# Batch 1's w1 and wo sums as transposed blocks on TensorE, with its kept heads at places 24 to 28 of the second pass

## The chip, the cores and the metric

The kernel runs on one core of one Trainium2 chip. The time is the device time of one execution in microseconds, from the first to the last instruction of that core; where several runs are compared, their median is meant.

## The reference

The reference is one decode step of a transformer block and all its gradients. There are B = 2 batch rows, D = 640, H = 32 heads of 128, caches of Sk = 4096 positions for each batch row and head, and Dff = 1728. Everything is bfloat16.

```python
def _fwd_reference(A_x, A_k_cache, A_v_cache, A_wq, A_wo, B_x, B_w1, B_w2):
    ...
    x = A_x
    h = x + _A_ref(_layernorm(x, axis=-1), A_k_cache, A_v_cache, A_wq, A_wo)
    h2 = h + _B_ref(_layernorm(h, axis=-1), B_w1, B_w2)
    return h2
...
_out, _vjp = jax.vjp(_f, A_x, A_k_cache, A_v_cache, A_wq, A_wo, B_w1, B_w2)
_grads = _vjp(grad_out)
```

`_A_ref` is attention of one query per head over its cache, and `_B_ref` is `relu(h @ w1) @ w2`. The outputs are the block's result and the gradients of x, of both caches, of wq, wo, w1 and w2. The two caches are read (128 MB in bfloat16), and gradients of the same size are written. For each head the gradient of V is an outer product of the softmax row with the incoming gradient `go`, and the gradient of K is an outer product of the score gradient with the query. The score gradient needs V times `go`, so V is read a second time once `go` is known.

`go` of a head is the matrix `wo` of that head times the gradient `gh1` of the middle row h. `gh1` in turn needs w1 times the gradient of the hidden layer. These two products, w1 (640 x 1728) times a vector and wo (4096 x 640) times a vector, are what the change moves.

## The kernel before

**Two passes over the heads.** The program is written out by a loop over a plan. Pass 1 (`p1_iter`) takes the 64 pairs of batch row and head in order: it transposes K tiles on TensorE (`transpose_group`, L415), forms scores and exponentials and sums V. Pass 2 (`p2_iter`) takes them in the order of a list `turns`: place j of this list is one turn. Pass 2 starts when batch 0 is known, while pass 1 still runs over batch 1; from place 13 on it runs alone.

**A turn of pass 2.** TensorE forms two row broadcasts (L844), then four groups of four float32 transposes of the V tile `Wt` (`pair_transpose`, L436), which ScalarE copies to SBUF (L441), and then the small products with `go` (`pair_matvec`, L449). VectorE makes the two gradient tiles in halves (`outer_half`, L822, named gV and gK), with a small `gsp` (L835) before gK. The GpSimd queue stores the two tiles of 1 MB (L879 for gV, L860 for gK). One V tile of 1 MB is loaded by the Sync queue (L457) for a later turn. For a turn, `bg_until` makes sure that the `go` of its head stands in the program before it.

**Kept heads.** The V tiles of the last 6 heads of batch 0 and the last 5 of batch 1 stay in SBUF from pass 1 (`KEPT`), so their turns in pass 2 need no load. They are the first places of each batch: 0 to 5, and 32 to 36.

**Buffers.** Twelve SBUF tiles of 1 MB have tags: "ld" for loads, "g" for gradients, "f" for finished weight gradients on their way out, "q" for wq and w2 tiles of the last stage. `give` hands a tile back, and `share(...)` sets how many each tag should have; a tile that is given back goes to a tag that lacks one. From place 36 on (`j >= H + KEPT[1] - 1`) the aim is 4 ld, 4 g, 3 f and 2 q. Loads are issued in a fixed order by `pump`, whenever an "ld" tile is free.

**Background work.** Three queues of generators are advanced a little after each step of a turn, each at a rate that is a sort of credit per step:

- the first (`middle_gen`) does the middle of the block for a batch row: the MLP, the w1 sums, `gh1`, and then the `go` groups of heads (`go_group`). For batch 1 it begins with place 13. Both sums are done on VectorE: the vector is spread over all partitions as a row (`bcast_cols`: TensorE products into PSUM, L633, and ScalarE copies, L636), and then `ttr` (L649) multiplies a block of w1 or a head of wo with this row and adds up along it.
- the second (`fin_gen`, rate RATE2) makes the gradients of w2, w1, wo and wq (`outer_rows`): products of two rows in bank tiles with the role "o" (L926), copies to a tile `ot` (L935 on ScalarE, and L933 on VectorE when `late` is set), and stores from the Activation queue.
- the third (`gx_gen`, rate RATE3) makes the gradient of x: once all `go` are done it loads wq tiles (`wqs`, L971), transposes them on TensorE (L993), copies them (L995) and multiplies (L1003).

The last two begin when the w1 sums of batch 1 are done, since their buffers take the place of w1. `mlp_out`, after the `go` groups, loads the w2 tiles and makes the block's result (L709).

**PSUM.** Transposes of both passes alternate between banks 0 and 1 ("tps"). "o" has banks 4, 5 and 6; while `gx_gen` accumulates, it holds bank 6.

Of the kernel before, what the change touches and what calls it, by code (L numbers as in the profile page):

```python
# [7 lines left out]
FP32 = mybir.dt.float32  # L8
# [7 lines left out]
def kernel(  # L16
# [34 lines left out]
    GT = 8  # L51
# [6 lines left out]
    def f_kc(c):  # L58
        return 128 if c < NFF else F_rem
# [332 lines left out]
    NP1 = len(pairs)  # L392
    KEPT = (6, 5)
    turns = [(b, h) for b in range(B) for h in (*range(H - KEPT[b], H), *range(H - KEPT[b]))]
    turn_of = {bh: j for j, bh in enumerate(turns)}
    kept = {(b, h) for b in range(B) for h in range(H - KEPT[b], H)}
    u_bank = [None]
# [256 lines left out]
    def turn():  # L654

        while slot[0] <= 0:
            yield 0.0
        slot[0] -= 1

    def one(src, b):  # L660
        return src[:, :, b]

    def go_group(b, h0, h1, hbc):

        hs = slice(h0, h1)
        n = h1 - h0
        go32 = small.tile([128, GH], FP32, tag="go32", bufs=1, name="go32")
        for k in range(n):
            yield from turn()
            ttr(wo_t[:, h0 + k, :], hbc[:], go32[:, k:k + 1], D)  # L670
            yield 0.9
        nc.vector.tensor_copy(out=goc[:, hs, b], in_=go32[:, 0:n])
# [20 lines left out]
        yield  # L693

    def mlp_out():

        ml32 = small.tile([128, ND, B], FP32, tag="ml32", bufs=1, name="ml32")
        nc.vector.memset(ml32[:], 0.0)
        for k in range(NW2):
            while free["q"] < 1:  # L700
                yield
            t = load_w2(k, "q", "(p c) d -> p c d")
            yield from wait(12)
            c1 = min(NF, (k + 1) * FP)
            m_ps = pst([128, ND, B], FP32, "mid", "mlp_ps")
            for c in range(ND):
                for cf in range(k * FP, c1):
                    kc = f_kc(cf)
                    nc.tensor.matmul(m_ps[:, c, :], lhsT=t[0:kc, cf - k * FP, c * 128:(c + 1) * 128],  # L709
                                     rhs=arow[0:kc, cf, :], start=(cf == k * FP), stop=(cf == c1 - 1))  # L710
            give(t)
            yield
            nc.vector.tensor_tensor(out=ml32[:], in0=m_ps[:], in1=ml32[:], op=ALU.add)
        ml_bf = small.tile([128, ND, B], BF16, tag="ml_bf", bufs=1, name="ml_bf")
        nc.vector.tensor_copy(out=ml_bf[:], in_=ml32[:])
        y_bf = small.tile([128, B, ND], BF16, tag="y_bf", bufs=1, name="y_bf")
        nc.vector.tensor_tensor(out=y_bf[:].rearrange("p b c -> p c b"), in0=h1c[:], in1=ml_bf[:], op=ALU.add)
        yield from wait(3)
        for b in range(B):
            store_row(y_bf[:, b, :], ND, out_0[b].rearrange("s (c p) -> (s c) p", p=128))  # L720
            yield

    def middle_gen(b):
        if o_next[0] < (b + 1) * H // OG:
# [44 lines left out]
        fbc = cols.tile([128, Dff], BF16, tag="fbc", name="fbc")  # L769
        gx2 = small.tile([128, 1, ND], FP32, tag="gx2", bufs=1, name="gx2")  # L770
        gx2p = small.tile([128, ND, 3], FP32, tag="gx2p", bufs=1, name="gx2p")
        FW = Dff // 3
        spread_f = bcast_cols(one(ghfc, b), NF, f_kc, fbc)
        have = 0
        for k in range(3):
            while have < min(Dff, (k + 1) * FW):
                next(spread_f)
                have += 512
                yield
            for c in range(ND):  # L780
                yield from turn()
                ttr(w1_t[:, c, k * FW:(k + 1) * FW], fbc[:, k * FW:(k + 1) * FW], gx2p[:, c, k:k + 1], FW)
                yield 0.85
        nc.vector.reduce_sum(out=gx2[:, 0, :], in_=gx2p[:], axis=AX.X)
        yield ("w1", b)
        yield from ln_bwd(gx2[:], x2c[:, :, b:b + 1], rstd2[:, b:b + 1], gc[:, :, b:b + 1], gh1c[:, :, b:b + 1], 1)
        hbc = cols.tile([128, D], BF16, tag="rowbc", name="hbc")
        yield from bcast_cols(one(gh1c, b), ND, lambda c: 128, hbc)
        yield ("gh1", b)

        first = H - KEPT[b]
        bounds = [(first, first + 2), (first + 2, H)] if b == 0 else [(first, H)]
        bounds += [(h, min(first, h + GH)) for h in range(0, first, GH)]
        for h0, h1 in bounds:
            yield from go_group(b, h0, h1, hbc)
        if b > 0:
            yield from mlp_out()

# [166 lines left out]
    def gx_gen(fin):  # L965
# [11 lines left out]
        for c in range(ND):  # L977
            while c >= len(tiles) or (step[0] < tiles[c][1] + 16 and not forced[0]):
                fetch()
                yield 0.0  # L980
            if acc is None:
                banks["o"].remove(6)
                acc = ps.tile([128, ND, B], FP32, tag="bank6", bufs=1, name="gx_ps")
            t = tiles[c][0]
            todo = list(range(H))
            prev = None
            for t0 in range(0, len(todo) + GT, GT):
                part = todo[t0:t0 + GT]
                nxt = None
                if part:  # L990
                    t_ps = pst([128, GT, 128], BF16, "tps", "t_ps")
                    for x, h in enumerate(part):
                        nc.tensor.transpose(t_ps[:, x, :], t[:, h * 128:(h + 1) * 128], ident_bf[:])  # L993
# [12 lines left out]
                prev = nxt  # L1006
# [50 lines left out]
    M0_ITERS = 7  # L1057
    P2_AT = H + 2 + M0_ITERS
    RATES = (0.2, 0.8, 0.2, 0.8, 0.45)
    RATE2 = 0.65  # L1060
    RATE3 = 0.45
    plan = []
    i = j = 0
    while i <= NP1 + 1 or j <= NP1:
# [60 lines left out]
    for n, (i, j) in enumerate(plan):  # L1125
# [4 lines left out]
            share(ld=KEPT[1] + 3, g=4)  # L1130
        if fin is not None and not bg2 and not bg3:
            share(ld=7, g=6)
        elif fin is not None and j >= H + KEPT[1] - 1:
            share(ld=4, g=4, f=3, q=2)
        if j is not None:
            while g2 is not None:
# [4 lines left out]
        if i is None and ("w1", 1) in done and fin is None:  # L1141
            wts.release()
            fin = tc.alloc_tile_pool(name="fin", bufs=1)
            big2 = tc.alloc_tile_pool(name="big2", bufs=1)
            more_home("f", big2)
            banks.update(sps=[2, 3], o=[4, 5, 6])
            bg2.append(("fin", fin_gen(fin)))
            bg3.append(("gx", gx_gen(fin)))
        late[0] = all(("go", B - 1, h) in done for h in range(H))
# [84 lines left out]
```

## Time and profile before

| what | value |
|---|---|
| time, median of 3 runs | 942.42 us (935.63 to 942.82) |
| span of the profiled run | 939.0 us, mean granted TensorE clock 0.778 |
| busy: PE, PE loads of weights, DVE, ACT, POOL | 82, 68, 70, 59, 15% |
| moved by DMA | 363.02 MB, mean 387 GB/s |
| HBM read, written | 212.16 MB, 149.13 MB |
| chain that ended last | PE 39%, DMA 29%, DVE 15%, ACT 10%, issue 5% |

Busy shares are of the whole span, and pass 1 and pass 2 have different limits, so they don't tell what one stage waits for. The chain's shares name what ended each wait. Two views by stage are of more use: the page's 40 slices of the span, and the table of stretches, which gives each engine's busy time, the granted TensorE clock, and the bytes moved per second between two times. Pass 2 starts at 271 us (the first L844), place 13 at 483 us, place 17 at 519, place 34 at 655 and the last place, 63, at 921 us.

### The profile page before, as it was taken

The page shows a single profiled execution, that of the slowest core. Times are in us where ns is not written, and L with a number is a line of the kernel's source. Part 1 is how long each engine was busy: PE and PEld are TensorE (multiplying, and loading weights), DVE is VectorE, ACT ScalarE, POOL GpSimd, SP SyncE. Part 2 cuts the span into 40 slices and gives each one's busy share as a digit, 9 for nine tenths or more (in the row PEclk, how much of TensorE's full clock was granted, in tenths as well). Part 3 has the DMA queues.
Part 4 walks back from the last instruction along what each step waited for, and adds up shares of the span by engine and source line. Part 5 has one row for each costly group of instructions (what it writes and reads, how often), then busy time and mean ns, then how long its engine had stood idle before and what let it go on. Part 6 is the DMA issues. An engine that isn't in the chain of part 4 may idle for free.

```text
span 939.0 us, 26775 instructions
## 1 busy us (share of the span) xinstructions
PE 766.9 (82%) x11482; PEld 641.4 (68%) x11482; DVE 661.9 (70%) x1237; ACT 551.0 (59%) x1162; POOL 141.0 (15%) x249
## 2 busy tenths in 40 slices
PE   6999898999998888988867838676988877887883
PEld 5878787888787777877757727564766665665652
DVE  4555677766876877786768889787797455465675
ACT  4666565667775776776633626444665564565652
POOL 1222111121001101010012112111121111021111
PEclk9999999999998999998886856556555575575556
DMA  8999999997878999999989999999999999999998
GB/s 348 418 399 410 406 394 410 412 418 266 308 280 341 360 389 423 425 422 414 419 328 369 405 426 395 395 391 376 397 406 398 425 425 423 354 389 377 333 423 364
DMA packets 59478, 363.02 MB, mean 387 GB/s; under 512 B 5696, under 2 KB 15552, under 8 KB 19168
## 3 DMA queue, kind: packets, MB, share of 16 engines
q1 hardware_dynamic: 37920, 212.18, 57.6%
q0 software_dynamic: 18432, 134.23, 34.7%
q10 hardware_dynamic: 3008, 14.91, 4.0%
q8 instruction: 90, 1.47, 0.6%
q14 instruction: 28, 0.23, 0.1%
HBM read 212.16 MB, written 149.13 MB: 385 GB/s over the span
## 4 chain that ended last, share of the span: by engine, by line
PE 39%; DMA 29%; DVE 15%; ACT 10%; issue 5%; POOL 0%; SPq 0%; POOLq 0%; DVEq 0%; ACTq 0%
DMA Kt<-in_A_k_cache_dram 12%; DMA out_dram<-gV 10%; PE t_ps L436 9%; PE m_ps L470 7%; PE t_ps L415 6%; ACT t_sb L420 5%; DMA out_dram<-gK 5%; DVE gV L822 5%; PE s_ps L426 4%; PE o_ps L926 3%; DVE gK L822 3%; DVE pk L477 2%; PE u_ps L495 2%; ACT t_sb L441 2%; DVE junk L649 2%
## 5 line engine op out<-in xcount | busy, mean ns | idle before, releaser
L420 ACT COPY t_sb<-t_ps 128x1024 bf16<-128x1024 bf16 x223 | 216.7, 1012 | 46.6 <-PE t_ps L415 41.8
L441 ACT COPY t_sb<-t_ps 128x512 f32<-128x512 f32 x256 | 149.9, 588 | 159.3 <-PE t_ps L436 156.4
L436 PE MATMUL t_ps<-ident_f,Wt 128*128 128x128 f32 x848 | 195.5, 378 | 3.7 <-ACT t_sb L995 1.4
L470 PE MATMUL m_ps<-pk,Vt 128*128 128x129 bf16 x2048 | 193.3, 224 | 1.0 <-DVE pk L477 0.6
L477 DVE TENSOR_TENSOR pk<-Kt,ep 128x2048 bf16<-128x2048 bf16 x128 | 156.3, 1221 | 34.6 <-ACT ep L520 34.5
L822 DVE TENSOR_TENSOR gK<-rb,gsp 128x2048 bf16<-128x2048 bf16 x128 | 152.2, 1224 | 32.2 <-DMA out_dram<-gK 20.1
L415 PE MATMUL t_ps<-ident_bf,Kt 128*128 128x128 bf16 x2048 | 156.8, 229 | 16.7 <-DMA Kt<-in_A_k_cache_dram 16.6
L822 DVE TENSOR_TENSOR gV<-rb,pp 128x2048 bf16<-128x2048 bf16 x128 | 152.7, 1218 | 23.3 <-DMA out_dram<-gV 20.2
L436 PEld LDWEIGHTS t_ps<-ident_f,Wt 128*128 128x128 f32 x848 | 135.8, 196 | 34.2 <-issue 23.5
L470 PEld LDWEIGHTS <-Vt 128*128 128x128 bf16 x2048 | 130.0, 100 | 29.1 <-issue 29.1
L415 PEld LDWEIGHTS <-Kt 128*128 128x128 bf16 x2048 | 129.3, 102 | 19.1 <-DMA Kt<-in_A_k_cache_dram 18.7
L449 PEld LDWEIGHTS <-t_sb 128*128 128x128 bf16 x2048 | 95.8, 106 | 40.1 <-ACT t_sb L441 18.5
L426 PE MATMUL s_ps<-qc,t_sb 128*128 128x1 bf16 x2048 | 89.2, 164 | 18.1 <-ACT t_sb L420 16.6
L449 PE MATMUL dp_ps<-gom,t_sb 128*128 128x2 bf16 x2048 | 95.2, 167 | 8.9 <-ACT t_sb L441 7.8
L426 PEld LDWEIGHTS <-t_sb 128*128 128x128 bf16 x2048 | 76.0, 97 | 30.6 <-ACT t_sb L420 27.4
L879 POOL DMA_DIRECT2D out_dram<-gV x64 | 34.2, 534 | 288.9 <-DVE gV L822 228.6
L860 POOL DMA_DIRECT2D out_dram<-gK x64 | 34.0, 531 | 279.8 <-DVE gK L822 224.7
L566 POOL COPY P_bf<-ep 128x32 bf16<-128x32 bf16 x40 | 42.6, 1065 | 220.1 <-ACT ep L520 220.1
L935 ACT CAST ot<-o_ps 128x512 bf16<-128x512 f32 (+4 forms) x134 | 60.2, 478 | 23.1 <-DMA out_dram<-ot 11.9
L561 DVE TENSOR_REDUCE rmax<-s_ps 128x1 bf16<-128x32 f32 x64 | 12.3, 193 | 61.4 <-PE s_ps L426 61.3
L649 DVE CUSTOM_DVE_ANT_0 junk<-wo_t,hbc 128x640 bf16<-128x640 bf16 x64 | 52.3, 817 | 0.2
L582 ACT CAST MT<-m_ps 128x128 bf16<-128x128 f32 x64 | 17.1, 267 | 59.1 <-PE m_ps L470 59.1
(194 smaller groups left out, 812.7 us busy)
## 6 DMA issues: line engine op xcount, KB each, us to landing
Kt<-in_A_k_cache_dram SPq DMA_DIRECT2D x64, 1024.0 KB, 14.2
Vt<-in_A_v_cache_dram SPq DMA_DIRECT2D x64, 1024.0 KB, 11.5
out_dram<-gV POOLq DMA_DIRECT2D x64, 1024.0 KB, 10.9
out_dram<-gK POOLq DMA_DIRECT2D x64, 1024.0 KB, 10.3
Wt<-in_A_v_cache_dram SPq DMA_DIRECT2D x53, 1024.0 KB, 10.8
wo_t<-in_A_wo_dram SPq DMA_DIRECT2D x4, 1280.0 KB, 14.1
wqs<-in_A_wq_dram SPq DMA_DIRECT2D x5, 1024.0 KB
wq_t<-in_A_wq_dram SPq DMA_DIRECT2D x5, 960.0 KB, 16.1
```

Of the source, the lines that this page charges most:

```text
L415: nc.tensor.transpose(t_ps[:, j, :], nat[:, g * GT + j, :], ident_bf[:])
L420: nc.scalar.copy(out=t_sb[:], in_=t_ps[:])
L426: nc.tensor.matmul(dst[:, sc:sc + 1], lhsT=t_sb[:, j, :], rhs=vec, start=True, stop=True)
L436: nc.tensor.transpose(t_ps[:, j, :], natf[:, 2 * cc:2 * cc + 2, :].rearrange("p c k -> p (c k)"), ident_f[:])
L441: nc.scalar.copy(out=t_sb[:], in_=t_ps[:])
L449: nc.tensor.matmul(dst[:, sc:sc + 2], lhsT=v[:, j, :, par], rhs=vecs[:, par, :], start=(par == 0), stop=(par == 1))
L470: nc.tensor.matmul(r["m"][:, 0:129], lhsT=r["V"][:, sc, :], rhs=r["pk"][sc // HALF][:, sc % HALF, 0:129], start=(sc == 0), stop=(sc == NSC ...
L477: nc.vector.tensor_tensor(out=p["pk"][k][:, :, 0:128].rearrange("p s (a two) -> p s a two", two=2), in0=p["K"][:, sl, :].rearrange("p s (a ...
L566: (nc.gpsimd if i < P2_AT else nc.vector).tensor_copy(out=P_bf[:, bhp, :], in_=ep[:, :, 0])
L649: nc.vector.tensor_tensor_reduce(out=junk[0:kc, 0:width], in0=in0, in1=in1, scale=1.0, scalar=0.0, op0=ALU.mult, op1=ALU.add, accum_out=acc)
L822: nc.vector.tensor_tensor(out=pairs_view(dst[:, sl, :]), in0=row.rearrange("p (a two) -> p a two", two=2)[:, None, :, :].to_broadcast([128 ...
L935: nc.scalar.copy(out=ot[0:P, k, n0:n0 + nn], in_=o_ps[0:P, 0:nn])
```

## The change

Four things change together.

1. For batch 1, the w1 and wo sums go to TensorE. `turned` transposes blocks of 128 x 128 of the weight (up to eight into one bank), lets ScalarE copy them, and one group later multiplies each with the column that holds the vector, accumulating in bank 6. `gx2_turned` does so for w1 (10 groups), `go_turned` for wo (32 groups, one for each head). Batch 0 keeps the sums on VectorE (`gx2_rows`, `go_group`). The row broadcasts for batch 1 go.
2. The five kept heads of batch 1 come at places 24 to 28 of the second pass, and the batch 0 heads that stood there come at 29 to 36.
3. The buffers are shared out anew from place 28 on in place of 36, so that "f" and "q" get theirs earlier.
4. RATE2 and RATE3, at which the second and third queue advance, are lower, so that this work, which begins earlier, is spread over more turns. "o" has two banks until `gx_gen` gives it bank 6.

In the program's order the w1 sums are then complete at place 19 (before: 22), the first `go` group of batch 1 at place 22 (26), the last at 33 (41); the first wq tile and the first w2 tile are asked for at place 33 (41), and `gx_gen` ends at place 53 (59). `fin_gen` ends at place 61 (60).

```diff
+    KEPT1_AT = 24
+    turns[KEPT1_AT:H + KEPT[1]] = turns[H:H + KEPT[1]] + turns[KEPT1_AT:H]
...
+    def turned(groups, cost):
+
+        prev = None
+        for parts in (*groups, None):
+            if prev is not None:
+                for x, (_, kc, dst, vec, first, last) in enumerate(prev[1]):
+                    nc.tensor.matmul(dst, lhsT=prev[0][0:kc, x, :], rhs=vec, start=first, stop=last)
+            if parts is not None:
+                t_ps = pst([128, GT, 128], BF16, "tps", "t_ps")
+                for x, (src, kc, *_) in enumerate(parts):
+                    nc.tensor.transpose(t_ps[0:kc, x, :], src, ident_bf[:])
+                t_sb = mats.tile([128, GT, 128], BF16, tag="XT", bufs=5, name="t_sb")
+                whole = sum(kc == 128 for _, kc, *_ in parts)
+                nc.scalar.copy(out=t_sb[:, 0:whole, :], in_=t_ps[:, 0:whole, :])
+                for x, (_, kc, *_) in enumerate(parts):
+                    if kc < 128:
+                        nc.scalar.copy(out=t_sb[0:kc, x, :], in_=t_ps[0:kc, x, :])
+                prev = (t_sb, parts)
+            yield cost
+
+    def go_turned(b, h0, h1):
+
+        acc = ps.tile([128, GH], FP32, tag="bank6", bufs=1, name="go_ps")
+        yield from turned([[(wo_t[:, h, c * 128:(c + 1) * 128], 128, acc[:, h - h0:h - h0 + 1],
+                             gh1c[:, c, b:b + 1], c == 0, c == ND - 1) for c in range(ND)]
+                           for h in range(h0, h1)], 1.2)
+        yield from go_done(b, h0, h1, acc)
...
+        if b == B - 1:
+            yield from gx2_turned(b, gx2[:, 0, :])
+        else:
+            yield from gx2_rows(b, gx2)
         yield ("w1", b)
...
-            yield from go_group(b, h0, h1, hbc)
+            yield from (go_group(b, h0, h1, hbc) if b < B - 1 else go_turned(b, h0, h1))
...
             if acc is None:
-                banks["o"].remove(6)
                 acc = ps.tile([128, ND, B], FP32, tag="bank6", bufs=1, name="gx_ps")
...
-    RATE2 = 0.65
-    RATE3 = 0.45
+    RATE2 = 0.58
+    RATE3 = 0.35
...
-        elif fin is not None and j >= H + KEPT[1] - 1:
+        elif fin is not None and j >= KEPT1_AT + KEPT[1] - 1:
             share(ld=4, g=4, f=3, q=2)
...
-            banks.update(sps=[2, 3], o=[4, 5, 6])
+            banks.update(sps=[2, 3], o=[4, 5])
```

More of the change, by code (lines that the diff above doesn't have):

```diff
@@ L663, in go_group @@
     def go_group(b, h0, h1, hbc):
-        hs = slice(h0, h1)
-        n = h1 - h0
         go32 = small.tile([128, GH], FP32, tag="go32", bufs=1, name="go32")
-        for k in range(n):
+        for k in range(h1 - h0):
             yield from turn()
@@ L671, in go_group, with go_done @@
             yield 0.9
+        yield from go_done(b, h0, h1, go32)
+    def go_done(b, h0, h1, go32):
+        hs = slice(h0, h1)
+        n = h1 - h0
         nc.vector.tensor_copy(out=goc[:, hs, b], in_=go32[:, 0:n])
@@ L693, in go_group, with gx2_turned @@
         yield
+    def turned(groups, cost):
[22 more added lines that the diff above has]
+        yield from go_done(b, h0, h1, acc)
+    def gx2_turned(b, gx2):
+        acc = ps.tile([128, ND], FP32, tag="bank6", bufs=1, name="gx2_ps")
+        yield from turned([[(w1_t[:, c, cf * 128:cf * 128 + f_kc(cf)], f_kc(cf), acc[:, c:c + 1],
+                             ghfc[0:f_kc(cf), cf, b:b + 1], cf == 0, cf == NF - 1)
+                            for cf in range(f0, min(NF, f0 + GT))]
+                           for c in range(ND) for f0 in range(0, NF, GT)], 0.8)
+        nc.vector.tensor_copy(out=gx2, in_=acc[:])
     def mlp_out():
@@ L721, in mlp_out, with gx2_rows @@
             yield
+    def gx2_rows(b, gx2):
+        fbc = cols.tile([128, Dff], BF16, tag="fbc", name="fbc")
+        gx2p = small.tile([128, ND, 3], FP32, tag="gx2p", bufs=1, name="gx2p")
+        FW = Dff // 3
+        spread_f = bcast_cols(one(ghfc, b), NF, f_kc, fbc)
+        have = 0
+        for k in range(3):
+            while have < min(Dff, (k + 1) * FW):
+                next(spread_f)
+                have += 512
+                yield
+            for c in range(ND):
+                yield from turn()
+                ttr(w1_t[:, c, k * FW:(k + 1) * FW], fbc[:, k * FW:(k + 1) * FW], gx2p[:, c, k:k + 1], FW)
+                yield 0.85
+        nc.vector.reduce_sum(out=gx2[:, 0, :], in_=gx2p[:], axis=AX.X)
     def middle_gen(b):
@@ L768, in middle_gen @@
         yield from wait(3)
-        fbc = cols.tile([128, Dff], BF16, tag="fbc", name="fbc")
         gx2 = small.tile([128, 1, ND], FP32, tag="gx2", bufs=1, name="gx2")
[L771 to L784, printed above, removed]
+        if b == B - 1:
+            yield from gx2_turned(b, gx2[:, 0, :])
+        else:
+            yield from gx2_rows(b, gx2)
         yield ("w1", b)
         yield from ln_bwd(gx2[:], x2c[:, :, b:b + 1], rstd2[:, b:b + 1], gc[:, :, b:b + 1], gh1c[:, :, b:b + 1], 1)
-        hbc = cols.tile([128, D], BF16, tag="rowbc", name="hbc")
-        yield from bcast_cols(one(gh1c, b), ND, lambda c: 128, hbc)
+        if b < B - 1:
+            hbc = cols.tile([128, D], BF16, tag="rowbc", name="hbc")
+            yield from bcast_cols(one(gh1c, b), ND, lambda c: 128, hbc)
         yield ("gh1", b)
```

## The prediction

> **What bounds the kernel now.** I read the page's slices first, because the change touches only one stage and its limit may differ from the average.
>
> ```profile
> PEclk9999999999998999998886856556555575575556
> DMA  8999999997878999999989999999999999999998
> GB/s 348 418 399 410 406 394 410 412 418 266 308 280 341 360 389 423 425 422 414 419 328 369 405 426 395 395 391 376 397 406 398 425 425 423 354 389 377 333 423 364
> ```
>
> Each slice is 23.5 us. The DMA row is nearly full everywhere, yet the bytes are not: 425 GB/s is the most that a slice moves, and 362 MB at 425 would be 854 us. So the 85 us above that are slices in which requests came too thinly. The slices 9 to 13 (before 330 us) lie ahead of the change. What the change can reach starts at slice 20. The granted TensorE clock halves there, too.
>
> Next I cut the second pass into stretches (columns after the times: busy us and count of PE, PEld, DVE, ACT, POOL; granted clock; DMA share; GB/s).
>
> ```profile
> 519.00:542.00 23.00, 19.21 (x278) 15.92 (x276) 20.75 (x35) 15.36 (x29) 3.92 (x9) 0.91 1.01 406
> 542.00:572.00 30.00, 11.23 (x111) 9.62 (x112) 25.88 (x45) 7.11 (x14) 4.93 (x10) 0.52 1.00 415
> 572.00:655.00 83.00, 60.70 (x590) 49.30 (x588) 68.11 (x121) 42.77 (x98) 14.01 (x30) 0.60 1.00 392
> 655.00:724.00 69.00, 59.34 (x535) 46.93 (x535) 58.35 (x98) 42.48 (x94) 14.20 (x29) 0.50 0.99 396
> 724.00:798.00 74.00, 59.34 (x595) 43.81 (x592) 40.16 (x47) 39.26 (x84) 9.14 (x21) 0.57 1.01 425
> 798.00:824.00 26.00, 21.99 (x201) 16.58 (x201) 12.01 (x17) 13.69 (x27) 1.83 (x4) 0.50 0.94 354
> 855.00:891.00 36.00, 30.20 (x265) 22.55 (x264) 20.07 (x31) 21.80 (x41) 4.70 (x11) 0.50 0.91 333
> 925.00:939.00 14.00, 0.00 (x0) 0.00 (x0) 4.91 (x5) 0.00 (x0) 1.59 (x3) 0.52 0.77 325
> ```
>
> I call 519 to 655 us (places 17 to 33) stage A and 655 to 939 stage B. In A, DVE is busy 114.7 of 136 us and DMA is full: the stage runs within 7% of the transfer rate. In B, DVE falls back and PE at half clock carries 80 to 86%; the transfer rate drops to 354 and 333 GB/s just where PE is fullest. The last 14 us are the last stores landing and stay.
>
> The chain of waits shows what a turn consists of there (start, us, what):
>
> ```profile
> 853.65 1.04 PE t_ps L436 x4
> 854.69 0.19 PE dp_ps L449 x8
> 854.88 0.54 PE o_ps L926
> 855.43 0.97 PE t_ps L993 x8
> 856.39 0.85 PE t_ps L436 x4
> 857.24 0.19 PE dp_ps L449 x8
> 857.43 0.54 PE o_ps L926
> 857.98 1.04 PE t_ps L436 x4
> 859.02 0.03 PE dp_ps L449 x2
> 859.05 6.29 DMA Wt<-in_A_v_cache_dram
> ```
>
> PE goes from one thing to the next without a gap until it meets a V tile that hasn't landed: its load could only be issued when an earlier turn's transposes gave the buffer back. A slow PE makes late loads, and late loads stop PE. L993 (the wq transposes) and L926 (the output products) are what is added to the plain turn here.
>
> **What the Trainium skill says.** "TensorE: Matmul & The Clock Gate", Part 4 (PE-mode transpose), says that the full clock doesn't engage for transposes. The trace agrees for the second pass: 59.34 of 69 us busy at clock 0.50. So I price added transposes at half clock. "ScalarE: Activation LUTs" (What ACT_TABLE_LOAD costs) gives 186 ns + 0.833 ns per element for an instruction with immediates: 1039 ns at 1024 elements, where this trace has 1012 (L420). "DMA: Bandwidth & Descriptors", Bandwidth, has 425 GB/s for a 16 MB transfer, which this trace reaches in 724 to 798 us.
>
> **The change, part by part.**
>
> *Removed from DVE.* 15 sums of w1 at 0.750 + 0.081 us and 32 of wo at 0.817 + 0.081 (L649 rows): 12.5 + 28.7 = 41 us between 525 and 705 us. About 32 us of it are in A. Also removed: the row broadcasts of batch 1, 4 + 2 ACT copies (2.1 + 0.9 us) and some 2 us of PE.
>
> *Added to PE.* w1: 5 row blocks of 14 columns, so 70 transposes and 70 one-column products; wo: 32 heads of 5 each. I take L993 and L1003 (the same code form) from the chain: 0.97 and 0.31 us for eight, at half clock. w1: 70/8 x 1.28 = 11.2; wo: 160/8 x 1.28 = 25.6; together 37 us. Bounds: at full clock the transposes would take about half (chain: L436 x4 is 0.85 at half clock, and the plain turns at 529 to 541 us, clock 1.00, took 3.9 to 4.6 us each), so some 20 us; with the waits of a crowded turn (below, x1.4) 52 us.
>
> *Added to ACT.* w1: 5 copies of 1024 (1.01), 5 of 640 and 5 of 64x128 elements; wo: 32 of 640. A 640-wide copy is between 0.588 (512, L441) and 1.012 (1024); the skill's price gives 0.72, which I take: 5.1 + 3.6 + 1.3 + 23 = 33 us. ACT goes from 65 busy of 136 us in A to about 95: it fits. PE waits for these copies one group later, with a whole step of work in between, so I cost that wait at nothing, unless ACT is itself behind.
>
> *A's sum on PE.* A plain turn is 4 x 0.85 + 4 x 0.19 + 0.24 = 4.4 us. I counted the products that the changed program has between the L844 pairs of one turn and the next, and priced them by the chain: places 17 to 33 rise from 96 to 134 us (91 us busy measured before, as part ran at full clock). The densest are 18 and 23 with 11.4 each. A turn of DMA in A is about 54 MB / 17 = 3.2 MB = 7.5 us. So PE comes up to the bound in A but hardly beyond: places 17 to 19 begin at full clock (0.91 above), and in 542 to 572 PE was idle 19 us while the stores drained; the 9 us more of places 22 and 23 go in there for nothing. Places 24 to 33 go from 62 to 76 us in a stretch of 83 us. DVE gets 32 us of air in the same stage, and the five kept heads need no V load at places 24 to 28, so A's transfers fall by some 3 MB (7 us). I put A at its old 136 us.
>
> *Kept heads and share, at nothing by themselves.* The bytes are the same. bg_until for head 27 is at place 24, its sum is ready at place 22 in the program's order, so nothing is forced. The four "ld" buffers come at place 31 in place of 39; four sufficed for 425 GB/s in 724 to 798 us. The "o" banks go from three to two in A: every L926 product waits for the copy two before it. Before, two served in 724 to 891 us. I give this 0 to 3 us and take 0, as there are only 36 such products in A.
>
> *wq, w2 and the lower rates.* This is where the gain would be. In B the program before stacks wq transposes on output products: places 50 to 56 have 66 us of PE work, up to 12.0 in one turn. After, the same places have 47; the wq work stands at places 35 to 49, at most 10.5 in a turn, and places 53 to 60 have 59 us for 71. B's total on PE is the same (216 and 213 us), only flatter. What can be won is what B lost against 425 GB/s: 69 us x (1 - 396/425) = 4.7; 26 x (1 - 354/425) = 4.3; 31 x (1 - 404/425) = 1.5 (824 to 855 us moved 404); 36 x (1 - 333/425) = 7.8; together 18.3 us. I take three quarters back, 14 us. The 7 us of transfers that A doesn't do come to B, but A then waits less for its stores; I let these cancel.
>
> Sum: 942.4 + 0 - 14 = 928 us.
>
> **The rivals.**
>
> *PE becomes the bound in A (slower).* For: in the crowded turns 50, 51, 55 and 56 a turn lasted (from one L844 pair to the next) 13.7 + 11.5 + 14.0 + 11.9 = 51.1 us for 41 us of priced PE work, 1.25 times as much; no stretch of the second pass has PE over 88% busy for long. 134 x 1.25 = 167 us, less what full clock and the idle 19 us take off (some 15), is 152 against 136. Then B's gain is halved by the 7 us that it takes over: 942 + 16 - 7 = 951 us; without any gain in B 958. Against: A's turns are mostly plain transposes, where PE has little to wait for.
>
> *The gain is a wash (same).* The crowding moves from places 50 to 56 to places 35 to 49, where all turns have 7.5 to 10 us of PE work, near 9.3 us of transfers (3.95 MB): the same starvation, elsewhere. Then A and B cancel: 941 us.
>
> *Both stages win.* If the denser PE work releases the clock more often, A runs at the transfer rate (51 MB, 120 us, and the 7 us go to B): 928 - 8 = 920 us.
>
> **How the numbers follow.** The forecast (928) has 0.38, both stages winning (920) 0.12, the wash (941) 0.18, PE bound (951 to 958) 0.32. Eight in ten lie from 914 to 957: it takes in the rivals, the two bounds for the added PE work, and leaves out the ends. Faster by over 1% (under 933): 0.50; within 1%: 0.19; slower (over 952): 0.31, since part of the PE-bound case lies within 1% and is balanced by the upper half of the wash.
>
> **What would show each step.** Right: L649 has no sums on w1 or wo after about 480 us; the new transposes cost near 0.97 us for eight at clock 0.5; A ends (place 34 begins) within 5 us of 655; no stretch of 25 us between 780 and 900 us lies under 380 GB/s; the last wq transposes are over before 850 us. Wrong: A's rate under 370 GB/s with PE over 90% busy, so the bound has moved to PE; or new holes in the GB/s row at places 35 to 49. If the clock stays at 1.0 through A, my price for PE was twice too high.

## The result, and the profile after

The changed kernel takes 971.87 us, median of 4 runs (967.0 to 977.89), beside 940.43 us for the kernel before (four runs, one more than in the table above). The ratio is 1.0344, 95% interval 1.0268 to 1.042. It is slower by 3.4%, where 928 us and a gain were forecast, and it lies outside the range. The profiled run spans 968.5 us, that of before 939.0.

The slices of the changed kernel (each 24.2 us; TensorE clock granted, DMA busy, bytes moved):

```profile
PEclk8999899999999999889955675666565557565756
DMA  9999999997888999999999698876999999889998
GB/s 350 420 399 408 397 391 411 412 412 273 300 313 330 357 412 423 412 424 396 374 378 382 224 425 342 350 286 249 422 423 420 404 390 401 357 341 419 422 395 350
```

There are new holes at slices 22 (224 GB/s) and 24 to 27 (down to 249). They are from 532 to 678 us, where the new sums stand. The later part looks as before, with a dip at slices 34 and 35.

To compare the two kernels I cut them by places. A place begins when TensorE forms the row broadcasts of its turn (L844 before, L895 after). Stage A is from the start of place 17 to that of place 34, stage B from there to place 63, and the rest is the last place and its stores. The table of stretches for A and B, first before (columns after the times: PE, PEld, DVE, ACT, POOL busy and count, clock, DMA share, GB/s):

```profile
519.30:654.70 135.40, 90.54 (x964) 74.24 (x961) 114.37 (x198) 65.22 (x139) 22.86 (x49) 0.64 1.00 400
654.70:920.70 266.00, 222.36 (x2089) 168.32 (x2087) 173.31 (x244) 154.88 (x315) 41.41 (x87) 0.54 0.98 395
```

and after:

```profile
517.80:677.10 159.30, 126.09 (x1442) 103.54 (x1440) 92.89 (x155) 94.51 (x190) 22.38 (x49) 0.65 0.82 316
677.10:946.50 269.40, 214.37 (x2050) 161.59 (x2048) 159.79 (x195) 148.06 (x301) 40.25 (x86) 0.58 0.99 400
```

Of the 29.5 us between the two profiled runs, A has 23.9, B 3.4, and the rest 3.6 (22.0 us for 18.4); places 0 to 16 have -1.5. In A, DVE is relieved, from 114 to 93 us, and PE goes from 91 to 126. The transfers fall from 400 to 316 GB/s. **No engine is full:** PE is busy 126 of 159 us, which is 79%, and DMA 82%. So the stage waits for something that a busy share doesn't show.

The first hole shows one such wait. Places 17 to 20 one by one, in the same columns:

```profile
517.80:529.50 11.70, 8.54 (x105) 7.13 (x103) 5.25 (x9) 5.78 (x10) 1.31 (x3) 0.65 1.00 369
529.50:545.20 15.70, 12.43 (x145) 10.45 (x143) 4.91 (x5) 8.95 (x16) 1.30 (x3) 0.50 0.68 265
545.20:550.50 5.30, 4.97 (x60) 4.54 (x57) 4.66 (x11) 2.82 (x5) 0.53 (x1) 0.62 0.13 53
550.50:556.40 5.90, 4.57 (x85) 3.97 (x83) 5.83 (x10) 4.27 (x9) 1.78 (x3) 1.00 1.00 304
```

Place 18 has 42 blocks of w1 to transpose. It takes 15.7 us, and toward its end DMA runs dry: in the next place it is busy 0.13 and moves 53 GB/s. The chain of waits inside place 18 (start, us, what):

```profile
533.44 0.80 PE t_ps L711 x6
534.24 1.05 PE t_ps L438 x4
535.28 0.19 PE dp_ps L451 x8
535.48 0.25 PE gx_ps L707 x6
535.73 0.98 PE t_ps L711 x8
536.75 0.04 issue
536.78 1.02 ACT t_sb L714
537.80 0.05 issue
537.85 0.37 PE gx_ps L707 x8
538.22 0.80 PE t_ps L711 x6
```

Compare it with the excerpt of before, where PE went from one thing to the next without a gap until a V tile was missing. Here two groups come one straight after the other. PE transposes eight blocks (0.98 us), waits 1.1 us for ScalarE to copy them, multiplies (0.37), and transposes the next six. Only then come the plain turn's own transposes (L438). The waits of stage A name who stands behind this (us in total, times, longest; POOL issues the stores):

```profile
POOL out_dram L911 <- DVE gK L873: 97.4, 17, 13.2
DVE gsp L886 <- PE dp_ps L451: 49.7, 12, 10.8
...
PE go_ps L707 <- ACT t_sb L714: 6.7, 8, 1.4
...
PE gx_ps L707 <- ACT t_sb L714: 6.3, 6, 1.2
```

The first of these rows in before:

```profile
POOL out_dram L860 <- DVE gK L822: 55.0, 16, 6.5
```

PE's own waits for the copies are 13 us. More waits stand behind them: DVE waits 49.7 us for the products L451 of the plain turn, up to 10.8 at once, so `gK` comes late and its store is issued late (97.4 us of waiting for 55.0). The buffer of the V tile goes back late as well, so its next load is late. In the same view of before, the row of `gsp` isn't among the 23 longest, of which the last is 2.2 us. The row is a sign of the loss and not its measure: f1 below, which is no slower than before, still has 25.9 us of it.

The first hole isn't the whole loss. The DMA share of A says that its transfers stood still for about 0.18 x 159.3 = 29 us; places 18 and 19 hold 10 of them. Places 30 and 31 hold 11 more, with only 5 and 10 blocks (f2 below comes back to them):

```profile
642.10:653.50 11.40, 8.01 (x78) 5.97 (x75) 5.25 (x7) 5.82 (x13) 1.31 (x3) 0.62 0.56 230
653.50:664.60 11.10, 9.56 (x86) 7.61 (x84) 6.20 (x14) 5.66 (x13) 1.30 (x3) 0.50 0.47 190
```

### The profile page after: what moved, and what is told of

Same layout as the page of the kernel before. It is cut to its first block, busy times and chain, and to the rows that moved or that the text cites. A ratio compares the mean times of both kernels' runs of the same rounds, so it can differ in the third digit from the quotient of the medians.

```text
span 968.5 us, 27632 instructions
## 1 busy us (share of the span) xinstructions
PE 794.5 (82%) x11923; PEld 663.6 (69%) x11923; DVE 630.6 (65%) x1148; ACT 573.6 (59%) x1198; POOL 140.4 (15%) x249
## 4 chain that ended last, share of the span: by engine, by line
PE 46%; DMA 22%; ACT 14%; DVE 11%; issue 5%; POOL 0%; ACTq 0%; SPq 0%; POOLq 0%; DVEq 0%
DMA Kt<-in_A_k_cache_dram 13%; PE t_ps L438 13%; PE m_ps L472 6%; DMA out_dram<-gV 6%; PE t_ps L417 6%; ACT t_sb L422 5%; PE o_ps L977 4%; ACT t_sb L443 4%; DMA out_dram<-gK 3%; PE s_ps L428 3%; DVE gV L873 3%; PE dp_ps L451 3%; DVE gK L873 2%; DVE pk L479 2%; ACT ot L986 2%
## 5 line engine op out<-in xcount | busy, mean ns | idle before, releaser
L438 PE MATMUL t_ps<-ident_f,Wt 128*128 128x128 f32 x848 | 196.0, 378 | 2.1 <-ACT t_sb L1045 1.0
L873 DVE TENSOR_TENSOR gV<-rb,pp 128x2048 bf16<-128x2048 bf16 x128 | 152.6, 1217 | 28.8 <-DMA out_dram<-gV 23.5
L417 PE MATMUL t_ps<-ident_bf,Kt 128*128 128x128 bf16 x2048 | 154.4, 226 | 15.4 <-DMA Kt<-in_A_k_cache_dram 15.3
L438 PEld LDWEIGHTS t_ps<-ident_f,Wt 128*128 128x128 f32 x848 | 135.3, 196 | 40.9 <-issue 31.0
L417 PEld LDWEIGHTS <-Kt 128*128 128x128 bf16 x2048 | 127.2, 101 | 17.9 <-DMA Kt<-in_A_k_cache_dram 17.6
L451 PEld LDWEIGHTS <-t_sb 128*128 128x128 bf16 x2048 | 96.8, 107 | 32.8 <-issue 12.5
L451 PE MATMUL dp_ps<-gom,t_sb 128*128 128x2 bf16 x2048 | 95.2, 167 | 5.1 <-ACT t_sb L443 4.8
L886 DVE SCALAR_TENSOR_TENSOR gsp<-dp_ps,negdot,P_bf 128x64 bf16<-128x64 f32 x64 | 17.9, 280 | 97.7 <-PE dp_ps L451 97.0
L986 ACT CAST ot<-o_ps 128x512 bf16<-128x512 f32 (+3 forms) x129 | 57.7, 473 | 3.4 <-PE o_ps L977 2.2
L563 DVE TENSOR_REDUCE rmax<-s_ps 128x1 bf16<-128x32 f32 x64 | 12.3, 193 | 62.9 <-PE s_ps L428 62.8
```

Source lines behind the costliest of these rows:

```text
L417: nc.tensor.transpose(t_ps[:, j, :], nat[:, g * GT + j, :], ident_bf[:])
L438: nc.tensor.transpose(t_ps[:, j, :], natf[:, 2 * cc:2 * cc + 2, :].rearrange("p c k -> p (c k)"), ident_f[:])
L451: nc.tensor.matmul(dst[:, sc:sc + 2], lhsT=v[:, j, :, par], rhs=vecs[:, par, :], start=(par == 0), stop=(par == 1))
L873: nc.vector.tensor_tensor(out=pairs_view(dst[:, sl, :]), in0=row.rearrange("p (a two) -> p a two", two=2)[:, None, :, :].to_broadcast([128 ...
L986: nc.scalar.copy(out=ot[0:P, k, n0:n0 + nn], in_=o_ps[0:P, 0:nn])
```

## The experiments

Sixteen variants were run. In the table, "ratio" is to the kernel before on the same chip, and A, B and rest are us of the profiled run, cut as above. The rows come from several chips, on which the kernel before took 938.8 to 940.4 us, so rows are compared by their ratios first. A profiled run can lie some us from the median: that of c2 took 948.0 us, that of a4 946.1.

| kernel | us | ratio, 95% interval | A | B | rest |
|---|---|---|---|---|---|
| before | 940.43 | 1 | 135.4 | 266.0 | 18.4 |
| after | 971.87 | 1.0344 [1.0268, 1.042] | 159.3 | 269.4 | 22.0 |
| a1_sums_only | 976.05 | 1.0379 [1.0294, 1.0463] | 178.7 | 256.4 | 21.5 |
| a2_w1_only | 946.68 | 1.0089 [1.0063, 1.0115] | 144.9 | 259.1 | 21.1 |
| a3_wo_only | 960.82 | 1.0223 [1.0154, 1.0292] | 155.8 | 263.7 | 21.0 |
| a4_rest_only | 940.76 | 1.0006 [0.9982, 1.003] | 136.5 | 268.5 | 16.9 |
| c1_lag2 | 962.52 | 1.0235 [1.02, 1.027] | 152.1 | 271.5 | 21.3 |
| c2_no_copies | 954.44 | 1.0146 [1.011, 1.0182] | 139.0 | 267.6 | 23.5 |
| d5_no_sums | 944.72 | 1.0045 [1.0025, 1.0065] | 131.2 | 272.9 | 21.0 |
| d3_dve_copies | 957.89 | 1.019 [1.0132, 1.0249] | 145.7 | 269.5 | 21.3 |
| e1_spread_lag1 | 956.75 | 1.0164 [1.0107, 1.022] | 150.0 | 262.4 | 21.4 |
| e2_sums_lag2 | 954.11 | 1.0174 [1.0125, 1.0223] | 158.3 | 252.8 | 21.4 |
| d1_lag2_spread | 942.06 | 1.0029 [1.0004, 1.0053] | 138.6 | 262.8 | 22.5 |
| d4_spread_dve | 940.06 | 0.9999 [0.9977, 1.0021] | 140.2 | 262.6 | 21.2 |
| f1_nosums_old_order | 940.69 | 1.0009 [0.9985, 1.0033] | 144.4 | 254.5 | 20.8 |
| f2_after_lag2_spread | 958.63 | 1.0165 [1.0101, 1.0229] | 143.6 | 273.6 | 20.2 |
| b3_after_warm | 987.24 | 1.0484 [1.0439, 1.053] | 160.5 | 284.2 | 21.8 |
| b4_before_warm | 950.22 | 1.0121 [1.0065, 1.0177] | 133.7 | 277.3 | 16.7 |

The edge between A and B is a place and not an amount of work. Where the w1 sums end sooner, background work moves from B to A, so A + B says more than A alone.

### Which part of the change: a1 to a4

a1 keeps both sums on TensorE and sets order, share and rates back; a2 and a3 do the same with one of the sums. a4 is the other way round: the sums on VectorE, all else as after (so "o" has two banks there, too).

```diff
a1, from after:
-    KEPT1_AT = 24
+    KEPT1_AT = H
-    RATE2 = 0.58
-    RATE3 = 0.35
+    RATE2 = 0.65
+    RATE3 = 0.45
a2, on top of a1 (wo back on VectorE, with its row broadcast):
+            yield from go_group(b, h0, h1, hbc)
a3, on top of a1 (w1 back on VectorE):
+        yield from gx2_rows(b, gx2)
```

a1: 

> Both sums of batch 1 on TensorE, as after; the order of the heads, the share of the buffers and the two rates as before ("o" with two banks, as bank 6 holds the sums). If the TensorE work in places 17 to 33 is the cost: 962 to 975 us, places 17 to 33 near 160 us. If the kept heads, the share or the rates are the cost: 938 to 945 us.

a2: 

> Only the w1 sums on TensorE, the wo sums on VectorE, all else as before. By TensorE work (11 of 37 us) a third of the loss: 948 to 954 us, with the hole at 530 to 545 us still there. If the wo sums alone are the cost: 938 to 943 us.

a3: 

> Only the wo sums on TensorE, the w1 sums on VectorE, all else as before. By TensorE work (26 of 37 us) two thirds of the loss: 955 to 965 us. If the waits of the w1 sums are the cost: 938 to 945 us.

a4: 

> The order of the heads, the share and the rates as after, both sums of batch 1 on VectorE (the sums of the five kept heads are then forced at place 24 if they aren't done). If TensorE is the cost: 930 to 945 us, or up to 5 us more by the forced sums. If the order, the share or the rates are the cost: 962 to 975 us.

The sums alone cost as much as the whole change: 36 us (a1), w1 7 and wo 21 of it; that the two together cost 8 more than their sum is within the intervals. a1 came 1 us above its range, with its stage A at 178.7 and not near 160; a2 came below the 948 to 954 of a share by TensorE work, with the hole still there (30 GB/s in its place 19). So this hole goes with a loss of only some 7 us. The order, the share, the rates and the two banks together cost nothing and bring nothing while VectorE has the sums: a4 lies within 0.3% of before. It also bears on the forecast's gain in B: a4 asks for its wq tiles from 693 to 796 us, before from 708 to 822, after from 676 to 783. Its stretches:

```profile
522.40:658.90 136.50, 97.15 (x973) 79.60 (x971) 121.92 (x218) 66.26 (x143) 24.45 (x50) 0.60 0.94 374
658.90:927.40 268.50, 217.56 (x2080) 162.65 (x2078) 166.88 (x224) 152.31 (x311) 40.77 (x88) 0.57 1.00 406
```

In B the rate is up from 395 to 406 GB/s, but B has more to move: 268.5 us x 406 = 109.0 MB for 105.1, and the 3.9 MB more are 10 us at the old rate. In A there is less to move and no time is won: it is at 374 GB/s and DMA share 0.94.

### What in the sums: c1, c2, d3, d5

c1 lets the products come two groups behind their transposes. c2 leaves the copies out: the products take the identity, and the true sums of batch 1 are not computed. d5 leaves out the transposes, too. d3 is c1 with the copies on VectorE. The main lines of the edits:

```diff
c1, in turned():
-        for parts in (*groups, None):
-            if prev is not None:
+        for parts in (*groups, None, None):
+            if len(waiting) == 2 or (parts is None and waiting):
+                t_sb, old = waiting.pop(0)
...
c2, in turned():
-                    nc.tensor.matmul(dst, lhsT=prev[0][0:kc, x, :], rhs=vec, start=first, stop=last)
+                    nc.tensor.matmul(dst, lhsT=ident_bf[0:kc, :], rhs=vec, start=first, stop=last)
-                nc.scalar.copy(out=t_sb[:, 0:whole, :], in_=t_ps[:, 0:whole, :])
...
d5, on top of c2:
-                    nc.tensor.transpose(t_ps[0:kc, x, :], src, ident_bf[:])
...
d3, on top of c1:
-                nc.scalar.copy(out=t_sb[:, 0:whole, :], in_=t_ps[:, 0:whole, :])
+                nc.vector.tensor_copy(out=t_sb[:, 0:whole, :], in_=t_ps[:, 0:whole, :])
...
```

c1: 

> The changed kernel with the products two groups behind the transposes, not one: the same work on every engine, but TensorE never waits for the copy it has just caused. If those waits are the cost (some 16 us of waits for the copies in the trace): 952 to 960 us. If TensorE's time itself is: 966 to 974 us.

c2: 

> The changed kernel without the ScalarE copies of the sums' transposes: the products take the identity as weights, so the sums of batch 1 are left out and TensorE's instructions stay as they are. If TensorE's own time is the cost: 960 to 972 us. If the 33 us on ScalarE and the waits for them are: 940 to 950 us.

d5: 

> The changed kernel without the transposes and the copies of the sums; the products remain, with the identity as weights (6 us of TensorE in all), so the sums of batch 1 are left out. What is left is the new order, share and rates with sums that cost next to nothing. If TensorE's time in the transposes is what remained when the copies went: 936 to 944 us. If taking the sums off VectorE is worth something by itself, as the prediction had it: 925 to 932 us. If something else of the change costs: over 948 us.

d3: 

> The changed kernel with the products two groups behind (962.5 us) and the copies of the sums' transposes on VectorE, which the change has relieved, in place of ScalarE. If ScalarE's time is the cost: 950 to 956 us. If VectorE's waits for stores now hold TensorE's products: 962 to 980 us.

Step by step from 971.9: without the wait for the copy just caused 962.5, without copies 954.4, without transposes 944.7. So of the 31 us, 9 go with that wait, 8 with what else the copies do, and 10 with the transposes. The intervals make each of these uncertain by 4 to 8 us. None of the four runs settled its question as it was put: c1, c2 and d3 came between their two ranges, d5 0.7 us above its first range. 4 us are left with nothing of the sums but the 230 one-column products, and VectorE doesn't have them either. In A alone the same steps read 159, 152, 139, 131, with c2's profile 6 us faster than its median. The copy on VectorE takes 0.49 us in place of 0.69 for 640 columns, but d3 and c1 can't be told apart, as their intervals overlap. What the copies do beside the wait isn't settled. A bank of `t_ps` is held until it is copied, and the plain turn's transposes share the two banks; c2 takes away both that and ScalarE's work.

### Crowding: e1, e2, d1, d4

In after and in a1, place 18 has 42 blocks and places 23, 26 and 29 have 25 each, five groups. The number of groups in a place follows from the price that each yields. e1 raises the prices, e2 has the lag of c1, d1 has both, each on a1; d4 is d1 with the copies on VectorE.

```diff
e1, on top of a1:
-                           for h in range(h0, h1)], 1.2)
+                           for h in range(h0, h1)], 1.7)
-                            for c in range(ND) for f0 in range(0, NF, GT)], 0.8)
+                            for c in range(ND) for f0 in range(0, NF, GT)], 1.2)
```

d1: 

> Both sums on TensorE, the order, share and rates as before (976 us with the products one group behind), with the products two groups behind and the groups spread over 22 turns, not 15. If the crowding of groups into a few turns is the cost: 945 to 955 us. If it is their number, wherever they stand: 962 to 970 us, as the waits alone give some 9 us.

d4: 

> The spread kernel with the copies on VectorE. If spreading and relief of ScalarE add up: 938 to 948 us, level with the kernel before. If VectorE's waits for stores hold the products: 955 to 975 us.

e1: 

> Only the spread, without the lag: as a1 (both sums on TensorE; order, share and rates of before), but a group's price in the rows is 1.7 (wo) and 1.2 (w1) in place of 1.2 and 0.8, which lays the groups over more turns; the products stay one group behind. a1 took 976.1 us, and with spread and lag together the kernel took 942.1. If the crowding of groups into few turns is the cause alone: 940 to 950. If the wait for the copy just caused matters in thin turns too: 952 to 968, and the lag is the larger part.

e2: 

> Only the lag, without the spread: as a1, with the products two groups behind their transposes. If crowding is the cause, with the wait a part of it: 960 to 970, as the lag alone took 9 us from the changed kernel (971.9 to 962.5). If the lag is enough where the order is that of before: 940 to 950.

It is both. From a1's 976.1 the spread alone takes 19 us, the lag alone 22, the two together 34 (by the ratios 20, 19 and 33). e1 came where thin places still pay the wait (952 to 968), but that the lag is the larger part isn't shown. d1 came 3 us below its better range. e2 came between the two cases, better than 960 to 970, without being enough. Its 22 us and c1's 9 can't be told apart by their intervals. With both, the groups lie over places 17 to 39, at most 15 blocks in a place after 18, and the sums cost 0.3%. d4 can't be told from d1. Stage A of a1:

```profile
519.90:698.60 178.70, 140.32 (x1449) 113.56 (x1446) 93.76 (x155) 99.26 (x198) 23.70 (x49) 0.56 0.82 314
```

and of d1:

```profile
517.10:655.70 138.60, 113.78 (x1342) 95.99 (x1339) 90.32 (x132) 88.67 (x182) 24.00 (x51) 0.68 1.00 400
```

The same kind of work in the same order moves at 400 GB/s in place of 314. PE is busy 27 us less in d1's A, more than the number of its instructions says (1342 for 1449, as some groups come after place 34, or 7%): the clock is 0.68 in place of 0.56. The chain in place 18 of d1 shows the new pattern:

```profile
527.29 0.48 PE t_ps L712 x8
527.77 0.02 issue
527.79 0.02 ACTq L715
527.81 0.04 issue
527.85 1.02 ACT t_sb L715
528.87 0.04 issue
528.91 0.61 PE t_ps L712 x6
529.52 0.59 PE t_ps L438 x4
530.11 0.18 PE dp_ps L451 x8
530.29 0.20 PE gx_ps L708 x8
530.49 0.58 PE t_ps L712 x8
```

Eight transposes take 0.48 to 0.58 us here, for 0.98 in the changed kernel: the clock is 1.00 in this place. The products (L708) come with no wait ahead of them. The copy at 527.85 is one for which the next six transposes wait; PE has the plain turn's work meanwhile, and the timeline shows it idle for only 0.26 us ahead of them. Lag and clock come together here. Place 18 of c1 has the same 42 blocks as after, with the longer lag; place 18 of e1 has d1's 34 blocks, with the short one:

```profile
524.40:533.80 9.40, 8.22 (x148) 7.20 (x145) 4.91 (x5) 8.32 (x16) 1.31 (x3) 1.00 1.00 376
531.40:543.60 12.20, 10.70 (x124) 8.89 (x122) 4.92 (x5) 7.28 (x13) 1.30 (x3) 0.50 1.00 381
```

After took 15.7 us for it at clock 0.50. So of the 6.3 us that the lag saves there, PE's busy time is 4.2 (12.43 to 8.22) and its idle time 2.1. The clock in place 18 is 0.50 where PE stops for the copies (after, a1, a2, e1; b3 with its extra products has 0.73), and 0.99 or 1.00 with two groups in flight (c1, d3, e2, d1, d4, f2) or without copies (c2). How much of d1's gain over the whole stage is the wait as such and how much the clock, no run separates.

### What the move could have brought at best: f1, and the cures in the changed order: f2

f1 is d5's edit on a1: no sums on either engine, in the order of before. As in d5, the true sums of batch 1 are left out. f2 is the changed kernel with lag and spread.

f1: 

> The sums of batch 1 left out (no transposes and no copies for them; the products take the identity), with the order, the share and the rates of before. Its output lacks the true go of batch 1. It bounds what any way of taking these sums off VectorE could bring. If VectorE's 41 us were what held stage A: stage A falls from 135 to 120 to 127 us, and the time to 925 to 934. If A was held by the transfers, as its 400 GB/s say: A stays at 130 to 136 us and the time at 937 to 944.

f2: 

> The changed kernel with both cures, the lag of two groups and the group prices 1.7 and 1.2, so the order of after in place of that of before. If the crowd was only a matter of the prices: 938 to 946, like d1. If the kept heads at place 24 force the groups together again, since their go must stand in the program by place 22: stage A keeps places of over 14 us, and the time is 950 to 962.

**f1 is as near to a ceiling as was tried, and it is where the kernel before already was:** 940.69 us, ratio 1.0009. Only the one-column products are left of the sums, and taking 41 us of work from VectorE was worth nothing. Its stage A is longer than expected, 144.4 us. The second queue starts sooner there (43 output products in A for 36 of before, PE 21.0 us busy on them for 13.1), and A moves 144.4 us x 390 = 56.3 MB for 54.2, which at 400 GB/s is 5 of the 9 us. B is shorter by 11.5, and A + B is 398.9 for 401.4.

f2 gives the time expected if the kept heads force the groups together, but not the mark for it: no place in A takes over 14 us. Place 24 does have 25 blocks again (10 in d1), places 24 and 25 take 12.3 and 13.0 us, and B has grown by 7.6 us over before. So with the cures the changed order costs 13 to 17 us over d1 (13 by the ratios), though a4 and d5, without groups on TensorE or without sums, put it at 1 to 4. Half of f2's loss is in A and half in B. What B's part comes from is left open.

For A, the traces show one thing that order and share may bring. The longest wait of the Sync queue, which issues the V loads, in stage A of after and then of before (us in total, times, longest):

```profile
SPq L459 <- PE t_ps L438: 117.3, 10, 46.3
SPq L457 <- PE t_ps L436: 107.5, 15, 20.2
```

In after this queue issues no V load from 623.2 to 669.9 us, from place 27 to place 32. The kept heads need none, and the new share gives "ld" tiles to "f" and "q". f2 has such a pause of 51 us, d5 one of 39, at the same places. In the order of before it lies at places 35 to 40 (39 us in before, 38 in d1), after most or all of the groups. From 625 to 670 us of after nearly all that moved was stores. Places 30 and 31, where its DMA engines idle, lie in the pause; in place 31 they idle in f2 and d5 as well (DMA share 0.45 and 0.53). So the change moved this pause to where its own groups stand. Whether the order or the share makes it, and how much of the loss is its own, no run separates.

### Buying the clock: b3, b4

b3 and b4 put an extra product of 128 x 512 ahead of each group of float32 transposes of a turn, from place 13 on, to raise the clock. Its result is overwritten.

```diff
-            g2 = p2_iter(j, 0)
+            g2 = p2_iter(j, int(i is None))
```

b3 (on after): 

> The changed kernel with one more product of 128x512 (its result is overwritten) ahead of each group of four transposes, from place 13 on. If the half clock is what makes TensorE the bound, and denser work holds the full clock: clock over 0.9 after 520 us and 935 to 955 us. If the clock stays at half, four products of 0.43 us a turn are added to a bound engine: over 1000 us.

b4 (on before): 

> The kernel before with the same extra products. If they hold the full clock, TensorE stops being the limit in places 34 to 60, and at most the 18 us lost there can come back: 920 to 940 us. If not: 960 to 1010 us.

The stretches of b3:

```profile
518.80:679.30 160.50, 130.64 (x1509) 103.84 (x1507) 92.73 (x155) 94.33 (x189) 22.41 (x49) 0.75 0.81 310
679.30:963.50 284.20, 228.59 (x2169) 164.76 (x2166) 160.63 (x195) 149.42 (x301) 38.45 (x86) 0.66 0.95 379
```

The clock rises, from 0.65 to 0.75 in A and from 0.58 to 0.66 in B, but PE's busy time rises too (126 to 131, 214 to 229). The extra products cost more than the clock gives back: 15 us in after, 10 in before. Both times fell between the two ranges, as the clock rose, but not to the 0.9 that b3's better range asked for.

## Why the prediction was wrong

**The PE work was priced well.** Eight transposes took 0.98 us, as taken (0.97), at clock 0.50. Over the stage the price was a little high, as part of it ran at full clock: the mean of a wo block is 264 ns, where a w1 block in place 18 has 308. The groups of the changed kernel by shape:

```profile
L714 ACT COPY t_sb<-t_ps 128x640 bf16<-128x640 bf16 x37 | 25.7, 695 | 19.0 <-PE t_ps L711 18.4
L711 PE MATMUL t_ps<-ident_bf,wo_t 128*128 128x128 bf16 x160 | 18.4, 264 | 0.0
L714 ACT COPY t_sb<-t_ps 128x1024 bf16<-128x1024 bf16 x5 | 5.1, 1012 | 3.7 <-PE t_ps L711 3.7
```

The 640-wide copy takes 0.695 us; the price of the Trainium skill ("ScalarE: Activation LUTs", What ACT_TABLE_LOAD costs) had given 0.72. With the 64-row copies (5 x 0.26) ScalarE's share is 32 us, as the 33 said. PE's busy time in A rose by 36 us, as the 37 said. No row of L649's sums (L651 after) is left after 480 us, as said.

**The step that failed first is "I cost that wait at nothing".** The step put "a whole step of work in between" a group's transposes and its products. In the crowded places groups come one straight after another, and then nothing is in between: PE waits 1.1 to 1.2 us for the copy it has just caused. c1 and e2 measured what a longer lag takes back: 9 us in the changed kernel, 22 in a1, with the clock that came with it.

**"I put A at its old 136 us" failed with it**, and is the larger error: 159.3. The working had the numbers to see it. It named places 18 and 23 as densest, with 11.4 us of PE work, and a place's transfers as 7.5 us. It then compared the sums over the stage, 134 with 136. The surplus of a crowded place need not be paid by the idle time of another, since loads and stores are issued from within each turn: place 18 took 15.7 us, 1.38 times its 11.4, and in the next one DMA was dry. (Place 23, with 25 blocks and 12.7 us, kept DMA full, so a crowded place doesn't always starve it.) That the arrangement is at fault more than the amount of work is shown by d1, where the same sums leave A at 138.6 and the whole at 942.

**The gain of 14 us in B** ("I take three quarters back") was 3 to 4 us, and the 7 us of transfers taken over from A ate it up. After moves 269.4 us x 400 = 107.8 MB in B for 105.1; at the old rate these 2.7 MB are 7 us, and B is only 3.4 us longer. "I let these cancel" failed because A won nothing back. Part of the reading behind this term was wrong as well: the rate was said to drop "just where PE is fullest", but the stretch with the highest PE share, 59.34 of 69 us, moved 396 GB/s, more than the two weak ones. (The floor of 854 us belongs to 363 MB, not 362.) The weak stretch stayed: from 830 to 855 us the transfers are at 308 GB/s, where no stretch under 380 between 780 and 900 was to be left. The last wq transposes ended before 850, as said (839.9). "The last 14 us ... stay" failed by a little: the rest after place 63 is 22.0 us for 18.4.

**That VectorE's 41 us would not shorten A** was right: the forecast put this gain at nothing, and f1 found none. **Kept heads, share and banks at nothing** were right with the sums on VectorE (a4), which isn't the kernel that was to be priced. With the sums on TensorE and both cures, order, share and rates cost 13 to 17 us (f2 against d1).

**The half clock** was right for the crowded places (0.50 in place 18), but not in general: d1 runs the same transposes at 1.00. "The trace agrees for the second pass" was read from one stretch. The first row of the same table has 0.91, with the transposes of plain turns in it.

**The rivals.** "PE becomes the bound in A" came nearest: its factor of 1.25 on crowded places gave 152 for A where 159 came, but its time, 951 to 958, is still short. Its mark was half fulfilled, the rate under 370 (316), but PE at 79% and not over 90. On this account PE bounds the stage by when it comes to the plain turn's work, and not by how much it has to do. The other sign, new holes at places 35 to 49, hardly came: the new holes are at places 18 to 33, and a dip like the one from place 49 on was there before. My objection to it, that "A's turns are mostly plain transposes", was an average where single places decide. "Both stages win" had denser work release the clock; the clock of A went only from 0.64 to 0.65.

## What to carry to other kernels

Before moving work to relieve an engine, leave that work out and look: here the move had nothing to win even so (f1), as the stage with the busiest VectorE moved at 400 GB/s with its DMA always busy. The parts of a change that cost nothing beside the old code (a4) are to be tried beside the new code, too: with both cures they cost 13 to 17 us (f2 against d1). Where an engine also has the work that each turn's transfers wait for, background work on it is to be compared place by place with the transfers of that place, and not summed over a stage. Where a group goes from TensorE over a copy and back, keep two groups in flight, and set their price so that few fall in one turn; the two cures together were worth 34 us here in the order of before, each alone about 20, but only 13 in the changed order.

## What was not expected of the hardware

The Trainium skill says that the full clock doesn't engage for transposes ("TensorE: Matmul & The Clock Gate", Part 4). In d1 it does, in a place whose work is nearly all transposes and products of one and two columns (524.3 to 532.0 us, the columns as in the stretches above):

```profile
524.30:532.00 7.70, 7.01 (x124) 6.29 (x122) 4.92 (x5) 6.93 (x12) 1.30 (x3) 1.00 1.00 364
```

The same transposes, place 18 of the changed kernel, ran at 0.50 with PE busy 12.43 of 15.70 us. In d1, PE is busy 91% of the time and in after 79%. But the busy share of a place doesn't decide it: place 20 of after ran at 1.00 with PE busy 4.57 of 5.90 us, and place 23 of c1, with 25 blocks of wo, at 0.50 with PE busy 99%:

```profile
563.80:576.80 13.00, 12.89 (x110) 9.38 (x108) 6.42 (x11) 8.40 (x17) 2.68 (x5) 0.50 1.00 401
```

What releases the clock, and what takes it back, stays open. That the clock matters to the transposes is plain: the mean of a w1 block is 0.22 us in d1's place and 0.31 in the other.
